# A cached-attention kernel whose TensorE loop is made to hold every pack, with two absent packs run on zeros first

## The chip, the cores and the metric

The kernel runs on one core of one Trainium2 chip. The metric is device time in microseconds of that core, lower is better. The profile is of one execution; its span starts with the first recorded instruction and is about 2 us shorter than the device time.

Words used below: a *pack* is two batches times four heads (128 packs in all); *j* is its place in a group of four packs; a *phase* is 32 packs that share one half of one block's `wq` and `wo`. "TensorE" is the profile's PE; "the DMA queue" is the one that SyncE (SP) issues all loads on. Packs are numbered from 0; the change adds packs -2 and -1, which do not exist.

## The reference

Two independent blocks A and B of attention with a given K and V cache, results side by side:

```python
B, Sq, D = 16, 64, 640
H, Sk, Dh = 32, 512, 128
q = (x @ wq).reshape(B, Sq, H, Dh).transpose(0, 2, 1, 3)
scores = einsum("bhqd,bhkd->bhqk", q, k_cache) * Dh ** -0.5
p = softmax(scores, axis=-1)
o = einsum("bhqk,bhkd->bhqd", p, v_cache)
return o.transpose(0, 2, 1, 3).reshape(B, Sq, H * Dh) @ wo
```

All inputs are bfloat16. The K and V caches of both blocks are 268 MB (4 x 16 x 32 x 512 x 128 x 2 bytes), and every byte is used once.

## The kernel before

A planner in Python lists every operation with an ideal time (`AT`, in packs), sorts them into one program per engine, and works out the semaphore waits. Each pack passes these stages on TensorE: `QP` (queries from x and wq), `S` (scores), `TR` (transposes of the normalized probabilities), `PV`, `OP` (output projection); once per group `XT` (transposes of x). `PV` and `OP` of pack n come about two packs after its `QP`, so TensorE's programme is software-pipelined.

```python
class Cfg:
    NK = 6          # K ring, packs
    NV = 4          # V ring, packs
    # ... cut ...
    PERIOD = 4
    FIRST = 4       # the hardware loop starts at pack 4
    PAD = 80
# ... cut ...
    lo = next(i for i, o in enumerate(pe) if o.kind == "QP" and o.idx == cfg.FIRST)
    hi = next(i for i, o in enumerate(pe) if o.kind == "QP" and o.idx == cfg.FIRST + cfg.PERIOD)
    size = hi - lo
# ... cut: waits of the loop are made periodic ...
        def run_program(e, eng, p):
            # ... cut: the other engines run their list straight ...
            for _ in range(0 if p else cfg.PAD):
                e.sem_inc(s_fl, 1)                 # padding, no one waits for it
            for op in prog[:lo]:                   # unrolled prologue: packs 0 to 3
                emit(e, op, p, {})
            with e.Fori(0, reps):                  # one turn: four packs
                # ... cut ...
            for op in prog[lo + size * reps:]:     # unrolled epilogue
                emit(e, op, p, taken)
```

The loads are sorted by deadline into one in-order queue. Its first entries are x of group 0, wq, K of pack 0 (first half), wq, K of pack 0 (second half), and then x of group 1, which must wait for `XT` of group 0, because the buffer for x has one slot:

```python
            op = add("sp", "LDX", g, txt - 0.5, [], [("xn", g % cfg.NXN)])   # NXN = 1
# ...
            loads.append((ready + 2.0 + 0.14 * PH * kt, ready, 1, op))       # wq of a later phase, spread
# ...
            ready = n - cfg.NK + AT["KT"][b] + 0.25 if n >= cfg.NK else -99.0
            loads.append((tk - 0.05, ready, 2, op))                          # K waits for a free slot
```

## Time and profile before

| | before |
|---|---|
| device time, median of 3 | 773.56 us (773.04 to 773.65) |
| span of the profiled execution | 770.5 us (device time 772.21, 1.35 us under the median) |
| loads | 292.06 MB, 97.1% of the DMA engines' time |
| TensorE busy | 685.8 us, 89% |

The page's strips of 40 slices (19.3 us each), and its lines for the queues. The first strip is the granted TensorE clock in tenths, the second the busy tenths of the DMA engines, the third what they moved.

```profile
PEclk9988799999999999999999999999999999999998
DMA  5999899999999999999999999999999999999960
GB/s 200 388 396 406 300 408 405 406 406 407 407 398 398 407 407 407 407 409 407 406 403 393 406 408 406 405 406 405 406 407 396 389 407 408 407 408 407 407 263 15
...
q1 hardware_dynamic: 97456, 292.06, 97.1%
q10 hardware_dynamic: 2304, 2.62, 1.0%
q8 instruction: 15, 0.25, 0.1%
```

The DMA engines are full from the second slice almost to the end, with three exceptions: the first slice, the fifth and the tail. At 406 GB/s the 294.7 MB of q1 and q10 (loads and stores) need 726 us (worked out from these lines), so a kernel that never let the DMA idle and had no tail would take that long. The change does not touch the tail.

The two weak places in stretches of 5 us. Columns after the engines' busy times are the granted clock, the DMA share and GB/s.

```profile
0.00:5.00 5.00, 0.00 (x0) 0.00 (x0) 0.00 (x0) 1.67 (x2) 0.94 (x7) 1.00 0.49 143
5.00:10.00 5.00, 0.00 (x0) 0.00 (x0) 1.25 (x1) 0.00 (x0) 2.44 (x2) 1.00 0.98 351
10.00:15.00 5.00, 0.69 (x5) 0.46 (x5) 1.25 (x1) 0.70 (x1) 0.29 (x1) 1.00 0.05 14
15.00:20.00 5.00, 3.74 (x52) 2.72 (x52) 1.34 (x2) 0.60 (x1) 2.83 (x3) 1.00 0.91 317
...
80.00:85.00 5.00, 2.25 (x126) 1.89 (x123) 0.06 (x1) 0.60 (x1) 0.72 (x2) 0.50 1.01 388
85.00:90.00 5.00, 4.01 (x77) 2.20 (x78) 0.80 (x2) 2.62 (x9) 0.00 (x0) 0.50 0.28 75
90.00:95.00 5.00, 5.00 (x220) 3.87 (x219) 3.14 (x6) 2.91 (x11) 2.69 (x4) 0.97 1.00 355
```

Two holes: 14 GB/s from 10 to 15 us, 75 GB/s from 85 to 90 us. The DMA queue's own waits name who was late. First those of the first 20 us, then those from 60 to 160 us:

```profile
SPq L516 <- PE ps L567: 10.0, 1, 10.0
...
SPq L539 <- PE ps L611: 63.6, 16, 10.9
```

The first line is the load of x of group 1 waiting for `XT` on TensorE. The second is K loads waiting until TensorE's `S` frees a K slot: 16 times, at longest 10.9 us. (What reads the slot is VectorE's transpose of K; the program takes `S`, which follows it, as the signal.) Why TensorE is late at the start is in the chain that ended last (start, length, what):

```profile
0.79 2.32 DMA xn_ring<-in_A_x_dram
3.11 10.10 issue
13.21 0.71 PE ps L567 x5
```

The data of x is there at 3.1 us, and TensorE starts at 13.2 us, with "issue" between: nothing that the profile shows as a wait. The trace has TensorE's semaphore instructions from 0.87 us on, one each 0.151 us: these are the 80 padding increments, 12.1 us together. Why TensorE is late at 85 us is in its timeline:

```profile
35.75 1.43 PE L611 MATMUL ps<-kt_ring,qs_ring 32*64 32x512 bf16 x17 [4.04 <-issue]
...
42.12 0.80 PE L690 MATMUL ps<-pT_sb,v_ring 32*128 32x64 bf16 x78 [0.69 <-issue]
...
48.16 0.38 PE L669 MATMUL ps<-ident,pn_sb 64*128 64x64 bf16 x14 [3.81 <-issue]
...
54.75 0.51 PE L690 MATMUL ps<-pT_sb,v_ring 32*128 32x64 bf16 x44 [1.60 <-issue]
```

Such stalls come in the middle of a stage, close to 128 matmuls apart (17 + 32 + 8 + 20 + 50 = 127 from the first to the second, 78 + 32 + 18 = 128 to the third); there are eight of them, of 0.7 to 4.0 us, between 31 and 86 us. The trace has a weight load for each matmul (26278 of both), so 128 of them are 256 instructions. On instruction queue q8 a packet of 16384 bytes ends 1.2 to 1.6 us before the end of each such stall, so I take this queue for TensorE's: eleven packets between 22 and 87 us, about 6.25 us apart but for the first two (10.9 us) and the last two (3.6 us). So what TensorE executed for the first time came here at 128 matmuls per 6.25 us while the data loads filled the DMA engines (busy share 1.03 to 1.05 between those packets); the same work at full speed takes about 3.3 us (128 of a turn's 821 matmuls, at 5.29 us a pack). Prologue (586 matmuls) and first turn of the loop (821) are such code, until about 88 us. In later turns the stalls are gone, and q8 has no packet from 87.1 to 757 us.

One rival has to be looked at: the granted TensorE clock also dips in this stretch, to 0.50 from 80 to 90 us. It does not set the pace of the blocks: from 39.6 us on they came 6.2 us apart at a mean clock of 1.00 (39.6 to 45.8 us) and 6.3 apart at 0.64 (64.7 to 71.0 us). The last two, 3.6 us apart, fall into the DMA's hole (232 GB/s between them), but whether the data loads hold the fetches back is not shown. How much the low clock added to the lateness once the last block was there is not separated.

### The profile page before, as it was taken

Reading aid. Unit: us, or ns where it says so; the run is one execution under the profiler, and the core shown is the slowest. Engines: PE = TensorE matmul, PEld = TensorE weight load, DVE = VectorE, ACT = ScalarE, POOL = GpSimd, SP = SyncE. Lnnn points to the kernel's source line nnn. Section 1 sums busy time; section 2 is a strip of 40 time slices with the busy share of each in tenths; the row PEclk is TensorE's granted clock in tenths of the full one; section 3 lists DMA queues with packets and bytes.
Section 4 is the critical chain, followed back from the end, with each engine's and each line's share of the span. In section 5 each row is a group of like instructions: output and inputs, shape, how many; then the busy total and the mean of one; then the engine's idle time right before and its main releaser. Section 6 shows DMA issues by size and latency. Waiting matters only on the chain.

```text
span 770.5 us, 56929 instructions
## 1 busy us (share of the span) xinstructions
PE 685.8 (89%) x26278; PEld 528.9 (69%) x26278; DVE 520.5 (68%) x806; ACT 517.8 (67%) x1554; POOL 405.0 (53%) x583
## 2 busy tenths in 40 slices
PE   1667699999999999999989989999999899899995
PEld 1455477777777777767767766777676676677774
DVE  1444477777777778767766677776777687677772
ACT  1444477777777777667767767777776676677773
POOL 3532355554694554544585544555578445455542
PEclk9988799999999999999999999999999999999998
DMA  5999899999999999999999999999999999999960
GB/s 200 388 396 406 300 408 405 406 406 407 407 398 398 407 407 407 407 409 407 406 403 393 406 408 406 405 406 405 406 407 396 389 407 408 407 408 407 407 263 15
DMA packets 99810, 295.22 MB, mean 383 GB/s; under 512 B 9264, under 2 KB 24112, under 8 KB 99760
## 3 DMA queue, kind: packets, MB, share of 16 engines
q1 hardware_dynamic: 97456, 292.06, 97.1%
q10 hardware_dynamic: 2304, 2.62, 1.0%
q8 instruction: 15, 0.25, 0.1%
q14 instruction: 35, 0.29, 0.1%
HBM read 292.03 MB, written 2.62 MB: 382 GB/s over the span
## 4 chain that ended last, share of the span: by engine, by line
SPq 34%; PE 29%; DMA 19%; POOL 7%; issue 6%; DVE 4%; ACT 1%; POOLq 0%; ACTq 0%; DVEq 0%
SPq L539 15%; DMA v_ring<-in_B_v_cache_dram 11%; SPq L548 10%; PE ps L690 7%; PE ps L710 6%; SPq L550 6%; POOL pn_sb L658 6%; PE ps L588 6%; PE ps L611 6%; PE ps L669 4%; DMA kn_ring<-in_A_k_cache_dram 2%; DVE pT_sb L676 2%; DMA v_ring<-in_A_v_cache_dram 2%; SPq L516 2%; DMA kn_ring<-in_B_k_cache_dram 1%
## 5 line engine op out<-in xcount | busy, mean ns | idle before, releaser
L658 POOL TENSOR_SCALAR pn_sb<-p_ring,recip 128x512 bf16<-128x512 bf16 x512 | 344.5, 692 | 337.9 <-DVE recip L645 337.9
L601 DVE STREAM_TRANSPOSE kt_ring<-kn_ring 128x1024 f32<-128x1024 f32 x256 | 307.4, 1225 | 67.8 <-DMA kn_ring<-in_B_k_cache_dram 37.2
L632 ACT ACTIVATE p_ring<-ps 128x512 bf16<-128x512 f32 x512 | 298.8, 598 | 38.0 <-PE ps L611 30.3
L676 DVE COPY pT_sb<-ps 128x1024 bf16<-128x1024 bf16 x256 | 164.2, 683 | 137.8 <-PE ps L669 137.5
L690 PE MATMUL ps<-pT_sb,v_ring 32*128 32x64 bf16 x14336 | 154.7, 193 | 27.5 <-DMA v_ring<-in_B_v_cache_dram 10.2
L588 PE MATMUL ps<-xT_ring,wqp_sb 128*128 128x128 bf16 x2560 | 168.7, 222 | 7.6 <-issue 4.5
L588 PEld LDWEIGHTS ps<-xT_ring,wqp_sb 128*128 128x128 bf16 x2560 | 159.6, 114 | 14.9 <-issue 4.8
L690 PEld LDWEIGHTS ps<-pT_sb,v_ring 32*128 32x128 bf16 x14336 | 140.2, 92 | 42.5 <-DMA v_ring<-in_B_v_cache_dram 16.8
L710 PE MATMUL ps<-wo_sb,oT_sb 128*128 128x320 bf16 x1024 | 165.1, 305 | 1.0 <-ACT ps L702 1.0
L698 ACT ACTIVATE oT_sb<-ps 128x256 bf16<-128x256 f32 x256 | 84.3, 381 | 115.3 <-PE ps L690 102.9
L611 PE MATMUL ps<-kt_ring,qs_ring 32*64 32x512 bf16 x4096 | 150.3, 404 | 5.6 <-issue 4.0
L669 PEld LDWEIGHTS ps<-ident,pn_sb 64*128 64x128 bf16 x4096 | 70.7, 96 | 85.8 <-ACT ps L702 51.2
L594 ACT ACTIVATE qs_ring<-ps 128x512 bf16<-128x512 f32 x128 | 76.5, 597 | 78.9 <-PE ps L588 78.4
L710 PEld LDWEIGHTS ps<-wo_sb,oT_sb 128*128 128x128 bf16 x1024 | 90.9, 99 | 38.7 <-ACT ps L702 1.2
L669 PE MATMUL ps<-ident,pn_sb 64*128 64x64 bf16 x4096 | 84.4, 192 | 25.1 <-POOL pn_sb L658 12.7
L632 ACT ACTIVATION_READ_ACCUMULATOR p_ring<-ps 128x1 f32 x512 | 106.5, 208 | 0.0
L611 PEld LDWEIGHTS ps<-kt_ring,qs_ring 32*64 32x64 bf16 x4096 | 56.2, 105 | 38.6 <-issue 8.0
L645 DVE RECIPROCAL recip<-rowsum 128x3 f32<-128x3 f32 (+1 forms) x256 | 38.0, 162 | 34.9 <-ACT p_ring L632 30.6
L702 ACT ACTIVATE ps<-zeros 128x256 f32<-128x256 bf16 x129 | 50.9, 395 | 0.0
L560 POOL COPY wqp_sb<-ws_sb 128x1280 bf16<-128x1280 bf16 x32 | 39.2, 1255 | 9.1 <-DMA ws_sb<-in_A_wq_dram 9.1
L567 PE MATMUL ps<-ident,xn_ring 128*128 128x128 bf16 x165 | 15.4, 227 | 13.2 <-issue 13.2
L577 POOL COPY xT_ring<-xs_sb 128x640 bf16<-128x640 bf16 x32 | 22.9, 716 | 6.2 <-ACT xs_sb L573 5.6
(20 smaller groups left out, 54.7 us busy)
## 6 DMA issues: line engine op xcount, KB each, us to landing
kn_ring<-in_A_k_cache_dram SPq DMA_DIRECT2D x128, 512.0 KB, 12.2
v_ring<-in_A_v_cache_dram SPq DMA_DIRECT2D x128, 512.0 KB, 12.0
kn_ring<-in_B_k_cache_dram SPq DMA_DIRECT2D x128, 512.0 KB, 14.7
v_ring<-in_B_v_cache_dram SPq DMA_DIRECT2D x128, 512.0 KB, 11.8
wo_sb<-in_A_wo_dram SPq DMA_DIRECT2D x8, 640.0 KB, 12.7
ws_sb<-in_B_wq_dram SPq DMA_DIRECT2D x10, 512.0 KB, 13.6
wo_sb<-in_B_wo_dram SPq DMA_DIRECT2D x8, 640.0 KB, 13.4
ws_sb<-in_A_wq_dram SPq DMA_DIRECT2D x4, 640.0 KB, 7.2
```

What stands on the lines that cost most here:

```text
L539: ins = e.dma_start(kn_ring[:, n % NK, b, :], src)
L548: ins = e.dma_start(dst.rearrange("p t d -> p (t d)"), src.rearrange("h (p t) d -> (h p) (t d)", t=16))
L588: last = e.matmul(ps[:, 1, f * 128:(f + 1) * 128], w[:, kt, f, :], xT_ring[:, xs, kt, :], start=(kt == 0), stop=(kt == KT - 1))
L601: ins = e.transpose(dst, kn_ring[:, n % NK, b, :].bitcast(F32))
L611: last = e.matmul(ps[64 * b:64 * b + 64, i, :], qs_ring[rows, n % NQ, f, b, :], kt_ring[rows, n % NKT, b, :, f // 2, :, f % 2], start=(f = ...
L632: ins = e.activation(dst, src, ACTF.Exp, scale=1.0, accum_out=rowsum[:, h:h + 1])
L658: ins = e.tensor_scalar(dst, src, recip[:, h // 4 % NR, i:i + 1], 1.0, ALU.mult, ALU.mult)
L669: last = e.transpose(pt_bank(b)[:, 64 * c:64 * c + 64], pn_sb[rows, c, :], ident[rows, rows], tile_position=(64 * b, 0))
L676: ins = e.tensor_copy(pT_sb[:, b].rearrange("p t q -> p (t q)"), pt_bank(b))
L690: last = e.matmul(ps[:, 4 + i, 64 * b:64 * b + 64], v_ring[rows, n % NV, b, c, :], pT_sb[rows, b, c, :], start=(t == 0 and i < 2), stop=(t ...
L698: ins = e.activation(oT_sb[:, 2 * a:2 * a + 2, :], o_ps[:, 2 * a:2 * a + 2, :], ACTF.Copy)
L710: last = e.matmul(out_ps[:, s, :], oT_sb[:, i, :], wo_sb[:, 4 * j + i, s * NH0:(s + 1) * NH0], start=(j == 0 and i == 0), stop=(j == NJ - ...
```

## The change

The intent: drop the padding and the prologue. TensorE goes into its loop after one `XT`, and the loop's first turn runs the late stages (`PV`, `TR`, `OP`) of packs -2 and -1 on buffers that were set to zero. The waits need made-up history, hence `BASE`, a count that the semaphores start at. The wq of the second phase is loaded soon instead of spread. Diff, cut to its core:

```diff
-    FIRST = 4
-    PAD = 80
+    BASE = 32
@@ one function adds the late stages of a pack, for n from -2 on
+    def add_output(n):
+        # ... cut: two lines ...
+        for b in range(2):
+            tv = n + AT["PV"]
+            op = add("sp", "LDV", (n, b), tv - 0.3, [], [("v", n % cfg.NV, b)])
+            ready = n - cfg.NV + AT["PV"] + 0.2 if n >= cfg.NV - 2 else -99.0
+            loads.append((tv - 0.05 if n >= 0 else -99.0, ready, 3, op))
+        # ... TR (not for -2), TE, PV, OE, ZO, OP, OS as before ...
@@ wq of the second phase
-            loads.append((ready + 2.0 + 0.14 * PH * kt, ready, 1, op))
+            loads.append((ready + 0.5 + 0.5 * kt if ph == 1 else ready + 2.0 + 0.14 * PH * kt, ready, 1, op))
@@ zeroed buffers
+    add("dve", "VZ", 0, -9.9, [], [("v", i % cfg.NV, b) for i in (-2, -1) for b in range(2)])
+    add("dve", "BZ", 0, -9.8, [], [("B", 4), ("B", 5), ("B67",)])
+    add("dve", "WZ", 0, -9.7, [], [("wo", NJ - 2), ("wo", NJ - 1)])
+    add("pool", "NM", -1, -1 + AT["NM"][3], [], [("pn", i) for i in range(4)])
@@ the loop starts at pack 0
-    lo = next(i for i, o in enumerate(pe) if o.kind == "QP" and o.idx == cfg.FIRST)
-    hi = next(i for i, o in enumerate(pe) if o.kind == "QP" and o.idx == cfg.FIRST + cfg.PERIOD)
+    lo = next(i for i, o in enumerate(pe) if o.kind == "QP" and o.idx == 0)
+    hi = next(i for i, o in enumerate(pe) if o.kind == "QP" and o.idx == cfg.PERIOD)
@@ a V load of an absent pack is only its semaphore increment, on the DMA queue
+            if n < 0:
+                return None, None
...
+            if last is None:
+                e.sem_inc(sem[op.sem], units(op.sem))
+                return
@@ before the loop
-            for _ in range(0 if p else cfg.PAD):
-                e.sem_inc(s_fl, 1)
+            for key in sorted(counts):
+                if key[0].startswith("q_"):
+                    e.sem_inc(sems[p][key], cfg.BASE)
```

The V "loads" of the absent packs have the deadline -99, so their increments stand first in the DMA queue; and the first of them waits for `VZ`, VectorE's memset of the two V slots. The queue is in order, so the first real load waits for that memset too: in the trace after, it issues at 5.48 us, where the memset ends at 5.18.

More of the change, by code (lines that the diff above doesn't have):

```diff
@@ L74, in add @@
         return op
+    def add_output(n):
+        g, j = n // NJ, n % NJ
+        final = n >= 0 and dims["FINAL"](g // NBP)
+        for b in range(2):
[3 more added lines that the diff above has]
+            loads.append((tv - 0.05 if n >= 0 else -99.0, ready, 3, op))
+        if n > -2:
+            add("pe", "TR", n, n + AT["TR"], [("pn", i) for i in range(4)] + [("ident",)], [("B", 4), ("B", 5)])
+        for b in range(2):
+            add("dve", "TE", (n, b), n + AT["TE"][b], [], [("B", 4 + b), ("pT", b)])
+        add("pe", "PV", n, n + AT["PV"], [("pT", 0), ("pT", 1), ("v", n % cfg.NV, 0), ("v", n % cfg.NV, 1)],
+            [("B", 4), ("B", 5), ("B67",)])
+        add("act", "OE", (n, 1), n + AT["OE"][0], [], [("B67",), ("oT", 1)])
+        add("act", "OE", (n, 0), n + AT["OE"][1], [], [("B", 4), ("B", 5), ("oT", 0)])
+        add("act", "ZO", n, n + AT["ZO"], [("zeros",)], [("B67",)])
+        add("pe", "OP", n, n + AT["OP"], [("oT", 0), ("oT", 1), ("wo", j)], [("B67",)])
+        if j == NJ - 1:
+            bp = g % NBP
+            add("dve", "OS", g, n + AT["OS"], [("acc", bp)], [("B67",), ("out_sb",) if final else ("acc", bp)])
+            if final:
+                add("act", "ST", g, n + AT["ST"], [("out_sb",)], [("out_dram", g)])
     if not general:
@@ L108, in build_plan @@
         add("pool", "PZ", 0, -9.95, [], [("zeros",)])
-    add("act", "ZO", -1, -9.8, [("zeros",)], [("B67",)])
-    for n in range(N):
+    add("dve", "VZ", 0, -9.9, [], [("v", i % cfg.NV, b) for i in (-2, -1) for b in range(2)])
+    add("dve", "BZ", 0, -9.8, [], [("B", 4), ("B", 5), ("B67",)])
+    add("dve", "WZ", 0, -9.7, [], [("wo", NJ - 2), ("wo", NJ - 1)])
+    add("pool", "NM", -1, -1 + AT["NM"][3], [], [("pn", i) for i in range(4)])
+    for n in range(-2, N):
+        add_output(n)
+        if n < 0:
+            continue
         g, j = n // NJ, n % NJ
-        ph = g // NBP
-        final = dims["FINAL"](ph)
         add("pe", "QP", n, n + AT["QP"], [("xT", g % cfg.NX), ("wqp", j)], [("SB", 1)])
@@ L121, in build_plan @@
             loads.append((tk - 0.05, ready, 2, op))
-            tv = n + AT["PV"]
-            op = add("sp", "LDV", (n, b), tv - 0.3, [], [("v", n % cfg.NV, b)])
-            ready = n - cfg.NV + AT["PV"] + 0.2 if n >= cfg.NV else -99.0
-            loads.append((tv - 0.05, ready, 3, op))
         add("pe", "S", n, n + AT["S"], [("qs", n % cfg.NQ), ("kt", n % cfg.NKT, 0), ("kt", n % cfg.NKT, 1)],
@@ L138, in build_plan @@
                 [("recip", n % cfg.NR, a)])
-        add("pe", "TR", n, n + AT["TR"], [("pn", i) for i in range(4)] + [("ident",)], [("B", 4), ("B", 5)])
-        for b in range(2):
-            add("dve", "TE", (n, b), n + AT["TE"][b], [], [("B", 4 + b), ("pT", b)])
-        add("pe", "PV", n, n + AT["PV"], [("pT", 0), ("pT", 1), ("v", n % cfg.NV, 0), ("v", n % cfg.NV, 1)],
-            [("B", 4), ("B", 5), ("B67",)])
-        add("act", "OE", (n, 1), n + AT["OE"][0], [], [("B67",), ("oT", 1)])
-        add("act", "OE", (n, 0), n + AT["OE"][1], [], [("B", 4), ("B", 5), ("oT", 0)])
-        add("act", "ZO", n, n + AT["ZO"], [("zeros",)], [("B67",)])
-        add("pe", "OP", n, n + AT["OP"], [("oT", 0), ("oT", 1), ("wo", j)], [("B67",)])
-        if j == NJ - 1:
-            bp = g % NBP
-            add("dve", "OS", g, n + AT["OS"], [("acc", bp)], [("B67",), ("out_sb",) if final else ("acc", bp)])
-            if final:
-                add("act", "ST", g, n + AT["ST"], [("out_sb",)], [("out_dram", g)])
     if not general:
@@ L170, in build_plan @@
         progs["sp"].append(e[3])
-        t_now += cfg.DMA_US[e[3].kind] / cfg.SLOT_US
+        if e[3].kind != "LDV" or e[3].idx[0] >= 0:
+            t_now += cfg.DMA_US[e[3].kind] / cfg.SLOT_US
     last_writer = {}
@@ L207, in build_plan @@
         if op.kind == "OP":
-            at[("OE", (op.idx, 1))].deps += [d for d in op.deps if d.kind == "LDWO"]
-            op.deps = [d for d in op.deps if d.kind != "LDWO"]
+            at[("OE", (op.idx, 1))].deps += [d for d in op.deps if d.kind in ("LDWO", "WZ")]
+            op.deps = [d for d in op.deps if d.kind not in ("LDWO", "WZ")]
         if op.kind == "XT" and op.idx > 0:
@@ L261, in stand_in @@
         raise RuntimeError(f"no stand-in for {d.kind} before {op.kind}")
-    counts = {}
+    base = {("q_" + eng,): cfg.BASE for eng in ("act", "dve", "pool")}
+    counts = dict(base)
     def sem_key(op):
@@ L280, in build_plan @@
         need[id(op)] = [e for e in (stand_in(d, op) for d in op.deps) if e is not None and e is not op]
-    order_waits(progs, need)
+    order_waits(progs, need, base)
     per = periodic_waits(progs, loop)
-    verify_waits(progs)
+    verify_waits(progs, base)
     loop["per"] = per
@@ L320, with __init__ @@
 class Clocks:
-    def __init__(self):
-        self.val = {}
+    def __init__(self, base):
+        self.val = dict(base)
         self.snap = {}
@@ L331, in learn @@
         for w in keep:
-            for s2, v2 in self.snap[w].items():
+            for s2, v2 in self.snap.get(w, {}).items():
                 if ck.get(s2, 0) < v2:
@@ L355, in wait_count, with order_waits @@
     return d.count + d.count % 2 if d.sem[0] == "d_v" else d.count
-def order_waits(progs, need):
-    ks = Clocks()
+def order_waits(progs, need, base):
+    ks = Clocks(base)
     def visit(eng, op):
@@ L407, in periodic_waits, with verify_waits @@
     return per
-def verify_waits(progs):
-    ks = Clocks()
+def verify_waits(progs, base):
+    ks = Clocks(base)
     def visit(eng, op):
@@ L486, in mha_kernel @@
                          for key in sorted(counts, key=str)})
-        s_fl = es.enter_context(nc.semaphore("s_fl"))
         NH0 = D // 2
@@ L510, in em_PZ, with em_VZ, em_BZ, em_WZ @@
             ins = e.memset(zeros[:, :], 0.0)
+            return ins, ins
+        def em_VZ(e, op):
+            ins = e.memset(v_ring[:, NV - 2:NV].rearrange("p n b t d -> p (n b t d)"), 0.0)
+            return ins, ins
+        def em_BZ(e, op):
+            ins = e.memset(ps[:, 4:8, :].rearrange("p e c -> p (e c)"), 0.0)
+            return ins, ins
+        def em_WZ(e, op):
+            ins = e.memset(wo_sb[:, HPH // 2:HPH, :].rearrange("p h n -> p (h n)"), 0.0)
             return ins, ins
@@ L543, in em_LDV @@
             n, b = op.idx
+            if n < 0:
+                return None, None
             blk, bp, j, h = pack_info(n)
@@ L650, in em_NM @@
             i = h % 4
+            if h < 0:
+                ins = e.memset(pn_sb[:, :, :].rearrange("p t c -> p (t c)"), 0.0)
+                return ins, ins
             if h // 4 % NJ in WIDE:
@@ L674, in em_TE @@
         def em_TE(e, op):
-            b = op.idx[1]
+            n, b = op.idx
+            if n == -2:
+                ins = e.memset(pT_sb[:, b].rearrange("p t q -> p (t q)"), 0.0)
+                return ins, ins
             ins = e.tensor_copy(pT_sb[:, b].rearrange("p t q -> p (t q)"), pt_bank(b))
@@ L716, in em_OS @@
             g = op.idx
-            sub = g // NBP % NSUB
+            sub = g // NBP % NSUB if g >= 0 else 0
             part = acc[:, g % NBP].rearrange("p (s c) -> p s c", s=2)
```

## The prediction

> **What bounds the kernel now.** The DMA queue. The page's parts 2 and 3 show 294.7 MB in 770.5 us; cut into stretches, the DMA moves 403 to 408 GB/s from 100 to 735 us. At 406 GB/s the bytes alone need about 726 us (my estimate). The rest is DMA idle at the start, one hole, and a tail: the last V load that holds TensorE lands at 719.6 us (chain that ended last); TensorE then needs 51 us at its own pace of about 5.28 us a pack.
>
> The start, in stretches of 5 us (GB/s): 143, 351, 14, 317, 365: about 10.3 us of DMA time lost. Cause: 80 padding semaphore increments on TensorE, 0.151 us apart, hold the first transpose of x until 13.2 us (its data landed at 3.1), and the second x load waits 10.0 us for it (the DMA queue's own waits). Second hole: 85 to 95 us runs at 75 and 355 GB/s, about 4.7 us lost. There TensorE is late: unrolled prologue and first loop turn are new code, and their 16 KiB instruction blocks come one per 6.25 us [...] (eleven such packets between 22 and 87 us; "issue" stalls of 2 to 4 us at every 128th matmul). So buffers come free late and the queue waits 10.9 us. [...]
>
> **What changes.**
> - The pads go: about -12 us for TensorE's start.
> - The prologue goes: 586 of 1407 matmul/weight-load pairs, about 4.5 blocks x 6.25 us. TensorE should reach the full-speed loop at about 53 us instead of 88, and pack 8's scores at 78 instead of 94. Added stages of absent packs: about 5 us warm, hidden in fetch-limited time.
> - New wait: the first DMA now waits for VectorE's zeroing of two V slots (8192 bf16 a partition, issued as 4096 words). [...] four semaphore increments on the queue, up to 0.6. First load at about 5.7 us instead of 0.8.
> - wq of phase two (2.6 MB) fills the queue while TensorE is fetch-limited. Bytes are unchanged.
>
> **On the critical path.** Only DMA idle time counts. Start: no hole at 10 to 15 us, but everything starts 4.9 us later: loss about 9.6 instead of 10.3. The hole at 85 to 95 us should vanish: -4.7. TensorE's other earliness turns into waits for V. Tail unchanged. Sum about -5.5 us: **768.0 us**, range **763.5 to 772.0** (8 in 10). Chances: faster by over 2% 0.03, within 2% 0.94, slower by over 2% 0.03.
>
> **What would show it.** First x load at 5 to 6 us; first transpose near 8; second x load near 9; no stretch of 5 us below 350 GB/s between 10 and 735 us; about seven 16 KiB packets before 60 us, none in the loop later; last DMA-bound V landing about 5 us earlier, then the same tail; more TensorE waits for V in the first phases.
>
> **What would make it wrong.** [...] The wo load that waits for the second absent pack's output projection (estimate 33 us, queue backlog then 6 us) could open a new hole. [...] Late phases may be limited by TensorE more than I think; then the gain is up to 12 us.

The forecast's sum is 0.7 us at the start and 4.7 at the second hole, put as about -5.5 us, so 768.0 us. The first load at 5.7 us, and with it the 4.9 us and the 9.6 us of the start, contain the memset's estimate, which rested on no trace; up to 0.6 us more are an estimate too, four increments at the 0.151 us of TensorE's pads. The "issue" stalls put at 2 to 4 us are 0.7 to 4.0 us in the trace. The 5 us of the absent packs' stages is an estimate: the page before has 1.2 us for a pack's `PV`, 1.3 for its `OP` and 0.7 for its `TR`, so 5.7 us for two, two and one of them.

## The result, and the profile after

| | before | after |
|---|---|---|
| device time, median | 773.61 us (773.04 to 774.21, 4 runs) | 766.76 us (766.11 to 767.44, 4 runs) |
| ratio to before | | 0.9911 [0.9894, 0.9929] |
| span of the profiled execution | 770.5 us | 764.1 us (device time 766.11) |
| TensorE's 16 KiB instruction packets | 15 | 10 |

Ratios here and below are the mean time of a kernel's fast runs over that of the other kernel's fast runs of the same rounds, with a 95% interval, so not quite the ratio of the medians quoted. The kernel before was run again beside each set; its median was 773.3 and 773.5 us in the later ones. The change is 0.9% faster, clear of noise.

The page's strips and queue lines of the kernel after:

```profile
PEclk9979999999999999999999999999999999999999
DMA  6999999999999999999999999999999999999960
GB/s 221 390 398 405 408 405 406 405 406 406 407 395 404 407 406 407 407 408 409 406 401 394 405 406 408 405 406 404 406 407 394 397 407 408 407 408 408 406 255 15
...
q1 hardware_dynamic: 97456, 292.06, 97.8%
...
q8 instruction: 10, 0.16, 0.1%
```

The weak fifth slice is gone (408 instead of 300 GB/s), the first is still weak, and the bytes are the same. The same stretches of 5 us:

```profile
0.00:5.00 5.00, 0.00 (x0) 0.00 (x0) 3.29 (x1) 1.28 (x1) 0.93 (x7) 1.00 0.00 0
5.00:10.00 5.00, 0.69 (x5) 0.46 (x5) 4.05 (x3) 0.70 (x1) 0.00 (x0) 1.00 0.61 167
10.00:15.00 5.00, 0.69 (x7) 0.72 (x8) 1.33 (x2) 0.00 (x0) 3.47 (x4) 1.00 0.99 345
15.00:20.00 5.00, 3.22 (x140) 2.98 (x141) 3.97 (x5) 0.60 (x1) 3.83 (x3) 1.00 1.07 400
...
80.00:85.00 5.00, 4.98 (x221) 3.81 (x219) 3.82 (x6) 3.86 (x13) 2.69 (x4) 1.00 1.02 409
85.00:90.00 5.00, 4.97 (x158) 3.79 (x156) 3.81 (x7) 3.89 (x14) 2.69 (x4) 1.00 1.03 410
90.00:95.00 5.00, 4.74 (x222) 3.76 (x219) 3.71 (x7) 4.05 (x14) 2.69 (x4) 1.00 1.03 411
```

The hole moved from 10 to 15 us to the very start: nothing is loaded in the first 5 us. The hole at 85 us is filled. Who was late in the DMA queue, first in the first 12 us, then from 60 to 160 us:

```profile
SPq L800 <- DVE v_ring L525: 4.5, 1, 4.5
...
SPq L539 <- PE ps L592: 0.6, 1, 0.6
...
SPq L573 <- PE ps L721: 12.8, 7, 4.1
SPq L562 <- PE ps L636: 12.5, 6, 3.0
SPq L575 <- PE ps L721: 7.2, 3, 3.2
```

The 10.0 us wait for `XT` has become 0.6 us, and in front of it stands a new wait of 4.5 us for the memset. From 60 to 160 us the waits for TensorE are still there, but none is over 4.1 us, and the DMA engines run through them (405 to 408 GB/s in the strip's slices from 57 to 172 us). The chain that ended last starts accordingly:

```profile
1.71 3.48 DVE v_ring L525
...
5.48 0.40 SPq L539
```

TensorE's timeline shows the same kind of stall as before, in fewer blocks (the fetches lie at 22.8, 30.0, 36.4, 42.6, 50.7 and 57.0 us, then none until 750 us):

```profile
32.41 0.58 PE L697 MATMUL ps<-ident,pn_sb 64*128 64x64 bf16 x27 [2.87 <-issue]
...
38.94 0.66 PE L721 MATMUL ps<-pT_sb,v_ring 32*128 32x64 bf16 x61 [2.72 <-issue]
...
45.24 1.76 PE L741 MATMUL ps<-wo_sb,oT_sb 128*128 128x320 bf16 x6 [3.63 <-issue]
...
53.24 0.56 PE L721 MATMUL ps<-pT_sb,v_ring 32*128 32x64 bf16 x27 [3.67 <-issue]
```

Where the time came from can be put in two ledgers, worked out from the two traces. The first is the DMA's lead: bytes landed on the load queue by a time, minus those of the kernel before, over 406 GB/s. The second is the pack's lead: how much earlier the first exponential of a pack starts.

| DMA lead at (us) | 10 | 20 | 30 | 80 | 90 | 95 | 200 | 400 | 600 | 700 |
|---|---|---|---|---|---|---|---|---|---|---|
| after, us ahead of before | -4.0 | 1.0 | 1.2 | 1.2 | 5.7 | 6.5 | 6.3 | 6.2 | 5.7 | 6.6 |

| pack | 0 | 3 | 4 | 8 | 16 | 32 | 40 | 48 | 72 | 96 | 112 | 127 |
|---|---|---|---|---|---|---|---|---|---|---|---|---|
| before, at us | 20.6 | 44.1 | 56.5 | 94.4 | 136.6 | 220.9 | 263.6 | 306.0 | 444.7 | 579.8 | 672.8 | 754.0 |
| after, us ahead | -1.6 | -11.7 | -5.6 | 11.2 | 11.2 | 11.1 | 10.4 | 6.6 | 6.7 | 6.8 | 6.6 | 6.5 |

The start gave 1.2 us, the hole at 85 us about 5 us, and nothing was gained or lost after 95 us. TensorE is first later than before (it starts with absent packs, on code that it has to fetch: six packets from 22.8 to 57.0 us), is 11.2 us ahead from pack 8 on, and loses that to 6.6 us between packs 40 and 48, where it begins to wait for V: TensorE's matmuls at `PV` were held up by V loads for 9.7 us between 210 and 400 us after, and 6.0 us before. The pace shows the change of regime: before, packs 8 to 48 come 5.29 us apart, packs 48 to 127 5.67. From there on both leads are the same, and so is the gain in the end.

### The profile page after: what moved, and what is told of

The parts are those of the page before. It is cut to its first block, busy times and chain, and to the rows that moved or that the text cites. A ratio compares the mean times of both kernels' runs of the same rounds, so it can differ in the third digit from the quotient of the medians.

```text
span 764.1 us, 57362 instructions
## 1 busy us (share of the span) xinstructions
PE 681.7 (89%) x26518; PEld 527.6 (69%) x26518; DVE 529.5 (69%) x814; ACT 518.8 (68%) x1559; POOL 406.7 (53%) x584
## 4 chain that ended last, share of the span: by engine, by line
SPq 38%; PE 28%; DMA 18%; POOL 6%; issue 5%; DVE 4%; ACT 0%; POOLq 0%; DVEq 0%; ACTq 0%
SPq L562 16%; SPq L573 11%; DMA v_ring<-in_B_v_cache_dram 8%; PE ps L721 7%; SPq L575 6%; PE ps L741 6%; PE ps L636 6%; PE ps L613 5%; POOL pn_sb L686 5%; DMA v_ring<-in_A_v_cache_dram 4%; PE ps L697 4%; DMA kn_ring<-in_A_k_cache_dram 3%; DVE pT_sb L707 2%; SPq L539 2%; DMA kn_ring<-in_B_k_cache_dram 2%
## 5 line engine op out<-in xcount | busy, mean ns | idle before, releaser
L721 PE MATMUL ps<-pT_sb,v_ring 32*128 32x64 bf16 (+1 forms) x14528 | 156.1, 192 | 34.0 <-DMA v_ring<-in_B_v_cache_dram 9.8
L721 PEld LDWEIGHTS ps<-pT_sb,v_ring 32*128 32x128 bf16 (+1 forms) x14528 | 141.7, 92 | 49.1 <-DMA v_ring<-in_B_v_cache_dram 16.2
L613 PE MATMUL ps<-xT_ring,wqp_sb 128*128 128x128 bf16 x2560 | 165.4, 220 | 5.6 <-POOL xT_ring L602 5.6
L613 PEld LDWEIGHTS ps<-xT_ring,wqp_sb 128*128 128x128 bf16 x2560 | 157.1, 114 | 11.9 <-issue 5.9
L636 PE MATMUL ps<-kt_ring,qs_ring 32*64 32x512 bf16 x4096 | 147.9, 399 | 0.0
```

The source lines that it names most:

```text
L613: last = e.matmul(ps[:, 1, f * 128:(f + 1) * 128], w[:, kt, f, :], xT_ring[:, xs, kt, :], start=(kt == 0), stop=(kt == KT - 1))
L636: last = e.matmul(ps[64 * b:64 * b + 64, i, :], qs_ring[rows, n % NQ, f, b, :], kt_ring[rows, n % NKT, b, :, f // 2, :, f % 2], start=(f = ...
L721: last = e.matmul(ps[:, 4 + i, 64 * b:64 * b + 64], v_ring[rows, n % NV, b, c, :], pT_sb[rows, b, c, :], start=(t == 0 and i < 2), stop=(t ...
```

## The experiments

The theory of the prediction was: time is DMA idle time; the start gains little because the memset takes the padding's place; the hole near 85 us closes because TensorE leaves the code that it has to fetch sooner. Rivals were that the early wq filled that hole, that the start does not count, and that the padding served nothing. Four kernels ran first, on one chip.

### Less padding alone

Edit of the kernel before:

```diff
-    PAD = 80
+    PAD = 48
```

> The kernel before with 48 padding increments instead of 80 [...]. My theory: time is DMA idle time; the first transpose moves from 13.2 to about 8.4 us, the second x load to about 9.1, before the queue runs dry at 10.2, so the hole at 10 to 15 us goes (about 4.4 us), while the hole at 85 to 95 us stays, since TensorE and the DMA move together: 768.8 us, 4.8 less than before. Rival (the start does not matter, only how soon TensorE reaches the loop with all code loaded): the hole near 85 us shrinks by the 4.8 us and the total is the same by another way; rival 2 (start hidden behind later DMA-bound stretches): 773.6.

Measured: 771.36 us (770.78 to 772.92, 5 runs), ratio 0.9970 [0.9957, 0.9983]. A miss: 2 us gained instead of 4.8. Stretches of the profiled execution (its slowest):

```profile
10.00:15.00 5.00, 3.63 (x50) 2.73 (x52) 2.52 (x3) 0.60 (x1) 2.94 (x3) 1.00 0.99 313
80.00:85.00 5.00, 1.06 (x91) 0.71 (x78) 0.57 (x1) 1.12 (x4) 1.39 (x3) 0.98 0.80 316
85.00:90.00 5.00, 3.77 (x61) 2.00 (x62) 0.86 (x2) 1.77 (x7) 0.00 (x0) 0.50 0.12 20
```

The first hole is gone as expected, and the DMA's lead is 4.8 us at 70 us. But it is 1.7 at 80, 0.1 at 90, and -0.1 at 100 us: in this execution the second hole grew by what the first had given. TensorE started 4.9 us earlier (pack 0), but that lead went in the fetches, three of which followed the one before by about 8 us instead of 6.25 (two show in the ends of its stalls, 45.08 to 53.06 and 65.59 to 73.13 us): 3.5 us are left at pack 3, 1.6 at pack 4, and -0.6 at pack 8. So what was loaded early filled the rings sooner, and then there was nothing to load. The step "TensorE and the DMA move together" was wrong. Why those fetches took longer is not settled; timed runs up to 2 us faster than the profiled one say that it varies. The ledgers compare a slow execution of this kernel (772.92 us) with a quick one of the kernel before (772.21 us), so they show the whole gain given back, where the medians keep 2.0 us of it.

### The early wq alone

Edit of the kernel before: the one line of the diff above that concerns wq.

> The kernel before with only the early load of the second phase's wq. My theory: the hole at 85 to 95 us is the queue with nothing it may load because TensorE is late; 1.5 MB more of wq before it fill it (about 3.9 us): 769.5 us, and the stretch from 85 to 90 us over 300 GB/s. Rival: the bytes are only moved from one full stretch to another and the hole stays: 773.6.

Measured: 770.19 us (768.94 to 772.36, 6 runs), ratio 0.9962 [0.9946, 0.9978]. The hole did mostly close as expected: 358 GB/s from 85 to 90 us instead of 75 (and 329 from 95 to 100), a DMA lead of 3.3 us at 95 us.

```profile
85.00:90.00 5.00, 3.01 (x73) 1.64 (x73) 0.00 (x0) 1.62 (x6) 0.00 (x0) 0.50 0.97 358
```

But of it 0.5 us is left at 150 us and 0.2 at 200 us. TensorE is no earlier (pack 8: 1.3 us later), so the loads that follow find no free slot sooner. The time agrees with the expectation; the way to it is not the one I gave. The two profiled executions differ by 1.9 us (770.26 and 772.21) and not by 3, and pack 127 is 1.0 us ahead in them; that lead arises between packs 48 and 56, where V begins to hold TensorE. I cannot say where the rest comes from.

### After, with wq spread as before

Edit of the kernel after: the same line put back.

> The kernel after with the second phase's wq spread as before. My theory: TensorE has left the fetch-limited code by 57 us, the queue's backlog is about 11 us then and drops to 5, so no hole opens: 766.8 us within 1 us of after. Rival (the early wq is what closed the hole at 85 us): a hole of about 4 us opens between 55 and 90 us and the time is about 771.

Measured: 767.09 us (766.55 to 767.79, 4 runs), ratio to before 0.9916 [0.9901, 0.9930], against 0.9911 of the whole change. DMA lead 5.6 us at 90 us, 6.2 at 200. No hole:

```profile
85.00:90.00 5.00, 4.96 (x159) 3.79 (x156) 3.87 (x6) 3.87 (x13) 2.71 (x4) 1.00 1.02 408
```

The early wq is worth nothing measurable in the kernel after; the rival falls.

### After, without the wait of the first load

Edit of the kernel after, so that the increments for the zeroed V slots stand behind the second x load:

```diff
-            loads.append((tv - 0.05 if n >= 0 else -99.0, ready, 3, op))
+            loads.append((tv - 0.05, ready, 3, op))
```

> The kernel after with the queue's markers for the two zeroed V slots put after the second x load, so that the first loads do not wait for VectorE's memset. My theory: the first load issues at 0.8 instead of 5.5 us and everything follows 4.7 us earlier, with no new hole: 762.1 us. Rival (the start is held by TensorE's instruction fetch or by the memsets in another way): little or no gain, 765 to 767.

Measured: 762.00 us (760.48 to 762.85, 5 runs), ratio to before 0.9849 [0.9835, 0.9863]. A hit to 0.1 us. The first load issues at 0.79 us:

```profile
0.79 0.40 SPq L539 DMA_DIRECT2D xn_ring<-in_A_x_dram  x1
```

The DMA lead is 5.9 us at 80 us, 10.8 at 100 and 10.9 at 200 us, and pack 127 is 10.7 us ahead. Here the start is kept in full, unlike in the first experiment, and TensorE is 15.1 us ahead at pack 8 (there -0.6). This is the fastest kernel, and beats both.

After these four the theory was changed: bytes loaded ahead are kept only if TensorE frees the ring slots ahead as well. A gain at the start and an earlier TensorE are worth something together only. Three more kernels tested that and the padding, again on one chip.

### Both cheap edits to the kernel before

Padding of 48 and the early wq: both holes are attacked without touching the loop.

> The kernel before with both 48 padding increments and the early wq, so with both DMA holes closed but TensorE as late as before (pack 8's exponential near 95 us). The theory of my prediction (only DMA idle time counts, each closed hole is kept): 4.4 + 4.5 us less, about 764.5. The theory revised after the first two experiments: bytes loaded ahead are kept only if TensorE frees buffers earlier; here it does not, so a DMA lead of 4 to 8 us near 90 us is given back by 200 us while the queue waits for TensorE: 770 to 771.5.

Measured: 769.61 us (769.27 to 771.93, 6 runs), ratio 0.9957 [0.9942, 0.9972]. The old theory's 764.5 is out of reach of any run; the new one's 770 is missed by 0.4 us, on the side of a larger gain. The stretches show the giving back:

```profile
85.00:90.00 5.00, 5.00 (x68) 2.72 (x53) 2.12 (x5) 2.42 (x8) 0.82 (x2) 0.50 0.81 298
90.00:95.00 5.00, 5.00 (x219) 3.96 (x217) 2.45 (x4) 2.78 (x9) 1.87 (x3) 0.94 0.25 88
...
140.00:150.00 10.00, 9.69 (x381) 7.53 (x366) 7.66 (x13) 8.16 (x25) 4.69 (x8) 1.00 1.03 373
```

The hole is not closed but pushed to 90 to 95 us (88 GB/s), and from 120 to 150 us the DMA runs at 373 to 393 GB/s while its queue waits for slots (64.0 us of waits for TensorE between 60 and 160 us, the longest 5.6). The DMA lead is 7.6 us at 90, 4.2 at 95, 2.3 at 150 us, and stays at 2.2 to 3.0. Pack 8 is 0.6 us ahead. So about two thirds of the lead were given back, not all of it, as I had expected.

### No padding at all

`PAD = 0` in the kernel before; correct.

> The kernel before without padding (wrongly placed loop on purpose). My theory: [...] its blocks are fetched again in every turn: over 150 packets of 16384 bytes on TensorE's instruction queue instead of 15, issue stalls in every turn, and over 850 us. Rival (the padding does nothing useful, and only delays the start): 15 packets and about 769 to 771 us.

Measured, one look (state unknown): 1383.83 us. The rival falls. The page's strip and its line for TensorE's instruction queue:

```profile
GB/s 353 401 228 236 191 202 213 167 243 188 246 208 188 278 206 204 232 175 243 196 256 215 189 254 266 199 197 217 212 244 236 181 234 186 219 190 189 206 142 46
...
q8 instruction: 285, 4.67, 1.4%
```

285 packets of 16384 bytes instead of 15, which is about 9 for each of the 31 turns, and the DMA never gets past about 280 GB/s after the first two slices while TensorE waits for its instructions (issue stalls before the matmuls of `QP` and `PV` alone add to 357 us). So the padding did serve something: with 80 increments before it the loop ran from 87.1 to 757 us without a packet; without them 285 came. With 48 the loop from 92 to 110 us shows no issue stall either, and the time was 771.36 us. Why the loop is fetched again without the padding is not shown; how many blocks it lies in was the author's estimate, and is cut from two expectations.

### After, with the first load later still

Edit of the kernel after: VectorE's memset of the V slots goes behind its two others.

```diff
-    add("dve", "VZ", 0, -9.9, [], [("v", i % cfg.NV, b) for i in (-2, -1) for b in range(2)])
+    add("dve", "VZ", 0, -9.6, [], [("v", i % cfg.NV, b) for i in (-2, -1) for b in range(2)])
```

> The kernel after with VectorE's memset of the V slots put behind its two other memsets, so that the first load issues near 10.1 instead of 5.5 us. My theory: once TensorE is early enough, a later DMA start counts one for one: about 4.6 us more, 771.4. Rival (TensorE is what bounds the total and its 11 us lead at pack 8 leaves slack): 767 to 768.

Measured: 771.73 us (770.58 to 773.59, 6 runs), ratio to before 0.9985 [0.9971, 0.9998]. The first load issues at 10.34 us, 4.86 us later than in the kernel after, and the median is 4.97 us longer. A hit.

```profile
10.34 0.40 SPq L539 DMA_DIRECT2D xn_ring<-in_A_x_dram  x1
```

With TensorE early (5.9 us ahead at pack 8), the start counts one for one; that about 5 of the change's 6.9 us can be lost by the order of three memsets shows how much rests on it.

## Why the prediction was right or wrong

The time was predicted as 768.0 us in a range of 763.5 to 772.0; 766.76 was measured. Point by point:

- **What bounds it.** Right. Bytes are the same, and after 95 us the DMA lead stays between 5.7 and 6.6 us.
- **The pads.** Right that they alone held the first transpose: it starts at 8.00 us after, as soon as x has landed ("near 8" was predicted), and the second x load issues at 8.72 ("near 9").
- **The new wait.** Right. First load at 5.48 us (5 to 6 predicted). The profile shows the memset (128 x 4096 uint32) as 3.47 us, but it starts at 1.71 us where VectorE was free from 0.74 on; from there to its end at 5.18 us are 4.4 us. The four increments on the queue took 0.06 us each, not up to 0.15.
- **The start in sum.** 0.7 us predicted, 1.2 measured. The stretch from 10 to 15 us ran at 345 GB/s, under the 350 that I had set as a floor. (So did 730 to 735, at 329, where the tail now starts sooner.)
- **The hole at 85 to 95 us.** 4.7 us predicted, about 5 measured (DMA lead 1.2 at 80 us, 6.2 at 100). That it closes because TensorE arrives sooner, and not by the early wq, is shown by spreading the wq again: 767.09 us.
- **TensorE's arrival.** Mis-sized. "Full-speed loop at about 53 us instead of 88, pack 8's scores at 78 instead of 94": it came to full speed at about 58 us, and pack 8's exponential starts at 83.2 us instead of 94.4, so 11.2 us ahead instead of 16. One packet came 8.1 us after the one before instead of 6.25 (42.6 to 50.7 us), and between 45 and 60 us, at a granted TensorE clock of 0.64 to 0.70, the matmuls were slower: 624 ns for one of `S` and 448 for one of `OP`, against 394 and 300 from 60 to 75 us at 1.00. The ledgers show no effect on the time: in the kernel after and in the runs with the first load earlier and later, the lead of the last pack (6.5, 10.7 and 1.6 us) is that of the DMA at 200 us (6.3, 10.9 and 1.4), not that of pack 8 (11.2, 15.1 and 5.9).
- **Instruction packets.** Seven before 60 us predicted, six found, and none in the loop later, as predicted.
- **The tail.** "Last DMA-bound V landing about 5 us earlier, then the same tail" is not what the chain shows: the last V on it lands at 707.8 us instead of 719.6, with 56.3 us after it instead of 50.9. It is a V of pack 118 instead of 119. The pack ledger, 6.0 to 6.6 us from pack 112 on, says what was meant, and is the better measure.
- **New holes.** The wo load that waits for the second absent pack's `OP` issued at 34.2 us (33 estimated), after a wait of at most 1.0 us, and opened none.

One step was too simple although the total came out: "Only DMA idle time counts." The first experiment and the fifth show that a hole can be closed and the gain still be lost (2 us left of 4.8; a DMA lead of 7.6 us that ends as 2.3). The second lost its DMA lead too (3.3 us, then 0.2), but its median kept 3.1 us, which the revised theory does not explain. What the change needs is both: a DMA that idles less, and a TensorE that frees K and V slots earlier, which points to the dropped prologue (32 padding increments fewer alone left TensorE no earlier at pack 8). In the kernel after TensorE had 11.2 us of lead to back 6.3 us of DMA lead, and so the simple sum held. The prediction had forecast such a lead (16 us), but did not make its sum depend on it; so far the total is luck. How small a lead would do is not tested: no run dropped the prologue and left the start as it was.

The largest thing that the change left lying is its own: the first load's wait for a memset that nothing needs before `PV` of pack -2 at 18 us. Moving it is worth 4.8 us, nearly as much again as the change.

## What to carry to other kernels

When a kernel is DMA-bound over its whole length, look for the stretches where the DMA is not full, and ask of each not only how to fill it but whether the consumer will free buffers early enough to keep what is gained. Code that TensorE executed for the first time came here at one 16 KiB block per about 6.25 us while the data loads filled the DMA engines, and took about twice its time at full speed (3.3 us): a shorter unrolled prologue was worth more than its instructions' busy time says. Look at what stands at the head of an in-order DMA queue: here a mere semaphore increment that waits for a memset delayed every byte behind it, at 4.8 us of the total.
